# The order of the first loads in a fused linear-attention and gated-FFN kernel: second x tile behind the first key-weight chunk, key products reordered to match

## The chip, the cores and the metric

The kernel runs on one core of a Trainium2 chip, in one launch. The metric is the device time of that launch in microseconds (us). The five engines of a core are named as in the profile: PE (TensorE, with PEld for its weight loads), DVE (VectorE), ACT (ScalarE), POOL (GpSimd) and SP (SyncE, which here only issues transfers). A q after a name (SPq, ACTq, PEq) means that engine's sequencer: instructions that issue a DMA or wait.

## What is computed

Shapes: x is 2048 rows of 640; wqkv is 640 x 1920; wo is 640 x 640; w_gate and w_up are 640 x 1728; w_down is 1728 x 640; all bf16. The part that matters here is the head of the linear-attention block, the projection of keys and queries.

```python
def _A_ref(x, wqkv, wo):                       # 32 heads of 20
    q, k, v = split(x @ wqkv)
    phi = lambda t: where(t > 0, t + 1, exp(t)) + 1e-6
    pq, pk = phi(q), phi(k)
    kv = einsum("bhsd,bhse->bhde", pk, v);  z = einsum("bhsd->bhd", pk)
    o = einsum(pq, kv) / (einsum(pq, z) + 1e-6)
    return o @ wo
def _B_ref(x, w_gate, w_up, w_down):
    return (gelu(x @ w_gate) * (x @ w_up)) @ w_down
g = sigmoid((x * gate_w).sum(-1))
out = g * _A_ref(x, ...) + (1 - g) * _B_ref(x, ...)
```

## The kernel before

The rows of x are cut into 16 tiles of 128 rows, the 640 columns into 5 chunks of 128 (KC = 5). A product of x with a weight needs x transposed (`xT`, one 128 x 128 block per tile and chunk) as the stationary operand and one weight chunk of 128 x 640 as the moving operand. Tiles 2 to 15 of `xT` come by a transposing DMA from SP (`load_xT`, L372). Tiles 0 and 1 are loaded plain (`load_x`, L345) and transposed by PE, so that PE can begin before any transposing DMA has landed.

**Who sets the order.** Each engine runs its own list in the order in which the program text records operations. A small planner, `_Plan`, turns the reads and writes that are declared for each operation into semaphore waits. An engine that waits holds up everything behind it in its list. DMAs are issued from two lists, SP's and ACT's; every load has a semaphore of its own. So the order of lines in the text is the order of the transfers on each queue and the order of the matmuls on PE.

**The loads.** `load_wk(k)` brings key chunk k (160 KB), `load_wq(k)` query chunk k (160 KB), `load_x(i)` x tile i (160 KB). SP issues x tile 0, wk 0, wk 1, wk 3, wq 0, wq 2, wq 4. ACT issues a tiny first DMA (`touch`, L355), x tile 1, then an `Exp` on one column that loads the activation table (L364), then wk 2, wk 4, the gate vector (1.2 KB, into `gw_sb`, which DVE has cleared at L367), wq 1, wq 3. Behind its loads SP issues the transposing loads of tiles 2 to 15; the first of these waits for wk 4 (L378). Then come the large weights of the later stages.

**The start of PE's list** (L502 to L524). `warm(c, n)` runs c matmuls of n columns on constants; they write bank 4 and nothing reads them. `T(i, ks, tb)` transposes chunks `ks` of tile i on PE into a PSUM bank and lets DVE copy them into `xT` (L431, L435). `KM(n, ks)` multiplies chunks `ks` of tile n with the key chunks: one matmul of 512 columns (L451) and one of 128 (L452) for each chunk, a "pair" below. Chunk 0 of a tile has a copy of its own, so that `KM(n, [0])` need not wait for the other four. `gate_col()` (L494) is one small matmul that makes the gate vector a column of `wq`. `QM` (L458) does the same as `KM` for queries of tiles 0 and 1. `phi1` and `phi2` are ACT's exponential and DVE's two steps.

```python
            warm(5, 512)
            warm(1, 128)
            T(0, [0], 7)
            T(0, [1, 2, 3, 4], 6)
            warm(6, 128)
            KM(0, [0])
            T(1, [0], 7)
            T(1, [1, 2, 3, 4], 6)
            warm(3, 128)
            KM(1, [0])
```

After these, chunks 1, 2, 3 alternate between the two tiles, then `gate_col()`, then chunk 4. From there on `KQ(i)` (L529) makes keys and queries of tiles 2 to 15 at once (L536, 15 matmuls per tile), `MM` (L586) the products of keys with x, `G` (L686, L697) the gate and up products of the FFN, and `O_tile` (L852, L861) the output.

Of the kernel before, what the change touches and what calls it, by code (L numbers as in the profile page):

```python
# [161 lines left out]
def bass_gated_mix__linear_attn_block__geglu_ffn__prompt_kernel(  # L162
# [63 lines left out]
    with (  # L226
# [8 lines left out]
        with contextlib.ExitStack() as stack:  # L235
            dma_sems = [stack.enter_context(nc.semaphore("s_in%d" % i)) for i in range(n_dma_in)]

            P = _Plan(["pe", "act", "dve", "pool", "sp"])
# [9 lines left out]
            def new_dma_key():  # L248
                k = "in%d" % dma_next[0]
                dma_next[0] += 1  # L250
                return k

            def v16(o, n):
                return pool[:, o:o + n]
# [45 lines left out]
            gw_sb = v16(O_GW, 128)  # L300
# [36 lines left out]
            r_gw = P.res("gw")  # L337

            def dma_in(dst, src, writes, reads=(), eng="sp"):
                P.op(eng, lambda e, dst=dst, src=src: e.dma_start(dst, src),  # L340
                     reads=reads, writes=writes, dma=new_dma_key())
# [3 lines left out]
            def load_x(i, eng="sp"):  # L345
                dma_in(x_aug[:, i, 0:640], A_x[0, i * 128:(i + 1) * 128, :], [r_xn[i]], eng=eng)

            def load_wk(k, eng="sp"):
                dma_in(wk[:, k, :], A_wqkv[k * 128:(k + 1) * 128, 640:1280], [r_wk[k]], eng=eng)

            def load_wq(k, eng="sp"):
                dma_in(wq[:, k, 0:640], A_wqkv[k * 128:(k + 1) * 128, 0:640], [r_wq[k]], eng=eng)
# [3 lines left out]
                 writes=[P.res("touch")], dma=new_dma_key())  # L356
            load_x(0)
            load_wk(0)
            load_x(1, "act")
            load_wk(1)  # L360
            load_wk(3)

            zero = nc.const_aps.tensor(0.0, (128, 1), F32)
            P.op("act", lambda e: e.activation(eg[:, 0:1], zero, ACT.Exp), writes=[r_eg[0]])  # L364
            load_wk(2, "act")
            load_wk(4, "act")
            P.op("dve", lambda e: e.memset(gw_sb, 0.0), writes=[r_gw])  # L367
            dma_in(gw_sb[0:5, :], gate_w.rearrange("(k p) -> k p", p=128), [r_gw], eng="act")
            for k in range(KC):
                load_wq(k, ("sp", "act")[k % 2])  # L370

            def load_xT(i, after=()):  # L372
                P.op("sp", lambda e: e.dma_start_transpose(xT[:, :, i * 128:(i + 1) * 128],
# [39 lines left out]
            def warm(count, n):  # L413
                def fn(e):
                    last = None
                    for w in range(count):
                        last = e.matmul(ps[:, 4, 0:n], one_l, one_r[:, 0:n], start=True, stop=True)  # L417
                    return last
                P.op("pe", fn, writes=[bank[4]])
# [4 lines left out]
            def slot(n):  # L424
                return SLOTS[n % 4]

            def T(i, ks, tb):
                def fn(e):
                    last = None
                    for n, k in enumerate(ks):  # L430
                        last = e.transpose(psb[:, tb, n * 128:(n + 1) * 128],  # L431
                                           x_aug[:, i, k * 128:(k + 1) * 128], ident)
                    return last
                P.op("pe", fn, reads=[r_xn[i], r_ident], writes=[bank[tb]])
                P.op("dve", lambda e: e.tensor_copy(  # L435
                    xT[:, ks[0]:ks[-1] + 1, i * 128:(i + 1) * 128],
                    psb[:, tb, 0:len(ks) * 128].rearrange("p (k s) -> p k s", k=len(ks))),
                    reads=[bank[tb]], writes=[r_xTa[i] if ks[0] == 0 else r_xT[i]])
# [4 lines left out]
            def KM(n, ks):  # L443
                i = seq[n][1]
                b0, b1 = slot(n)

                def fn(e):
                    last = None
                    for k in ks:
                        lhs = xT[:, k, i * 128:(i + 1) * 128]  # L450
                        e.matmul(ps[:, b0, :], lhs, wk[:, k, 0:512], start=(k == 0), stop=(k == KC - 1))  # L451
                        last = e.matmul(ps[:, b1, 0:128], lhs, wk[:, k, 512:640],  # L452
                                        start=(k == 0), stop=(k == KC - 1))
                    return last
                P.op("pe", fn, reads=[r_xTa[i] if i < NXN and ks == [0] else r_xT[i]] + [r_wk[k] for k in ks],
                     writes=[bank[b0], bank[b1]])
# [37 lines left out]
            def gate_col():  # L494

                P.op("pe", lambda e: e.matmul(ps[:, 7, 0:5], gw_sb, ident[:, 0:5], start=True, stop=True),
                     reads=[r_gw, r_ident], writes=[bank[7]])
                P.op("dve", lambda e: e.tensor_copy(wq[:, :, 640:641], ps[:, 7, 0:5].unsqueeze(2)),
                     reads=[bank[7]], writes=[r_gcol])
# [4 lines left out]
            warm(1, 128)  # L504
            T(0, [0], 7)
            T(0, [1, 2, 3, 4], 6)
            warm(6, 128)
            KM(0, [0])
            T(1, [0], 7)
            T(1, [1, 2, 3, 4], 6)  # L510
            warm(3, 128)
            KM(1, [0])
            for k in (1, 2, 3):
                KM(0, [k])
                KM(1, [k])
            gate_col()
            for k in (4,):
                KM(0, [k])
                KM(1, [k])
            for n in range(4):  # L520
                if n == 2:
                    for k in range(KC):
# [403 lines left out]
```

## Time and profile before

| what | value |
|---|---|
| plain runs, median of 4 | 274.19 us (273.76 to 274.64) |
| profiled execution, its own time | 274.27 us |
| its span, first to last instruction | 273.0 us |
| PE busy | 268.9 us, 98% |
| DVE / ACT / POOL busy | 141.8 / 76.0 / 30.0 us |
| granted TensorE clock, mean | 1.0 |
| first matmul (a constant one) | 0.82 us |
| first transposes of tile 0 / of tile 1 on PE | 3.10 / 4.97 us |
| first key pair, tile 0 / tile 1 | 4.48 / 5.83 us |
| first query matmul / first matmul of `KQ` | 8.48 / 11.20 us |

The issue time of each of the first loads, read from the timeline of its queue, and the time to landing, read from the DMA issues of a window that holds this load alone:

| load | queue, place | issued | to landing |
|---|---|---|---|
| x tile 0 | SP 1 | 0.79 | 2.3 |
| x tile 1 | ACT, behind touch | 1.23 | 3.3 |
| wk 0 | SP 2 | 1.26 | 3.1 |
| wk 1 | SP 3 | 1.71 | 3.7 |
| wk 2 | ACT | 1.78 | 3.8 |
| wk 3 | SP 4 | 2.18 | 3.9 |
| wk 4 | ACT | 2.19 | 4.1 |
| wq 0 | SP 5 | 2.66 | 4.1 |
| gate vector | ACT | 2.69 | not given |
| wq 2 | SP 6 | 3.13 | 4.8 |
| wq 1 | ACT | 3.31 | 4.8 |
| wq 4 | SP 7 | 3.60 | 5.4 |
| wq 3 | ACT | 3.69 | 5.4 |
| xT tile 2 | SP, after wk 4 landed | 6.33 | 3.8 |

How to read it: a load has landed at the sum of the last two columns. A matmul's duration in the profile is longer than the distance to the next one, since matmuls overlap; the pace of PE is read from the distance between starts.

### The profile page before, as it was taken

The numbers are of one execution on the slowest core, as the hardware profiler recorded it, in microseconds if no ns is written. First come the engines' busy times: TensorE is split into PE (matmuls) and PEld (weight loads), VectorE is DVE, ScalarE is ACT, GpSimd is POOL, SyncE is SP. The second block draws the span as 40 slices with busy tenths as digits, with TensorE's granted clock in tenths as the row PEclk, the third lists the DMA queues.
The fourth block names the chain that finished last, engine by engine and source line by source line (L and its number), as shares of the span: only waits on it lengthen the run. The fifth ranks groups of instructions, "written<-read, shape, count | busy, mean of one in ns | idle before, by whom it ended". The sixth has DMA issues, their size and how long they took to land.

```text
span 273.0 us, 3426 instructions
## 1 busy us (share of the span) xinstructions
PE 268.9 (98%) x1343; PEld 129.1 (47%) x1369; DVE 141.8 (52%) x251; ACT 76.0 (28%) x132; POOL 30.0 (11%) x28
## 2 busy tenths in 40 slices
PE   8999999999999999999999999999999999999997
PEld 5555555544445444444444444444444444444444
DVE  2598988998234334999999999634210000000200
ACT  2455554310421453223222223224011121121021
POOL 5000000003240001242332422000000000000000
DMA  7876999500300011522221221263031110110211
GB/s 232 166 107 120 341 402 383 130 3 11 66 19 2 23 50 50 184 43 48 26 48 24 48 43 33 58 206 119 5 77 38 41 38 19 38 41 19 58 58 41
DMA packets 42208, 23.61 MB, mean 86 GB/s; under 512 B 31567, under 2 KB 40783, under 8 KB 42063
## 3 DMA queue, kind: packets, MB, share of 16 engines
q1 hardware_dynamic: 41429, 22.56, 31.2%
q10 hardware_dynamic: 762, 0.82, 0.8%
q8 instruction: 11, 0.18, 0.3%
q14 instruction: 6, 0.05, 0.1%
HBM read 13.83 MB, written 2.63 MB: 60 GB/s over the span
## 4 chain that ended last, share of the span: by engine, by line
PE 96%; DVE 2%; issue 1%; ACT 1%; DVEq 0%; ACTq 0%
PE ps L697 41%; PE ps L861 23%; PE ps L536 12%; PE ps L593 6%; PE ps L840 4%; PE ps L808 2%; PE ps L675 2%; PE ps L596 2%; PE ps L417 1%; PE ps L451 1%; PE ps L821 1%; PE ps L466 1%; DVE pool L490 1%; PE ps L718 1%; DVE pool L555 1%
## 5 line engine op out<-in xcount | busy, mean ns | idle before, releaser
L697 PE MATMUL ps<-pool 128*128 128x512 bf16 x510 | 113.0, 379 | 0.5
L697 PEld LDWEIGHTS ps<-pool 128*128 128x128 bf16 x520 | 50.5, 98 | 60.0
L861 PE MATMUL ps<-pool 128*128 128x512 bf16 (+2 forms) x300 | 62.4, 366 | 0.3
L703 ACT ACTIVATE pool<-ps 128x512 f32<-128x512 f32 x52 | 31.1, 597 | 73.1 <-PE ps L697 73.1
L705 DVE TENSOR_TENSOR pool<-ps,pool 128x512 bf16<-128x512 f32 x52 | 34.7, 689 | 31.7 <-PE ps L697 30.3
L861 PEld LDWEIGHTS ps<-pool 128*128 128x128 bf16 x306 | 29.2, 98 | 33.4 <-issue 0.4
L536 PE MATMUL ps<-pool 128*128 128x512 bf16 (+1 forms) x206 | 37.9, 343 | 0.2
L844 DVE TENSOR_TENSOR pool<-ps,pool 128x512 bf16<-128x512 f32 x4 | 2.8, 692 | 61.5 <-PE ps L840 61.5
L751 POOL TENSOR_TENSOR pool<-pool 128x640 f32<-128x640 bf16 x16 | 22.5, 1408 | 72.8 <-DVE pool L753 65.7
L868 ACT ACTIVATE pool<-ps,pool 128x512 bf16<-128x512 f32 (+1 forms) x16 | 10.9, 681 | 68.6 <-PE ps L861 68.6
L536 PEld LDWEIGHTS ps<-pool 128*128 128x128 bf16 x210 | 20.5, 98 | 17.5
L555 DVE SCALAR_TENSOR_TENSOR pool<-ps,pool 128x128 bf16<-128x128 f32 (+2 forms) x42 | 25.3, 603 | 2.4
L546 ACT ACTIVATE pool<-ps 128x640 bf16<-128x640 f32 x28 | 19.7, 704 | 18.1 <-DVE pool L555 10.6
L593 PE MATMUL ps<-pool 128*128 128x512 bf16 x76 | 19.2, 379 | 0.1
L761 DVE TENSOR_TENSOR pool<-pool 128x640 bf16<-128x640 bf16 x16 | 13.2, 825 | 0.6
L759 DVE TENSOR_SCALAR pool<-pool 128x32 f32<-128x32 f32 x16 | 12.9, 803 | 0.6
L753 DVE TENSOR_REDUCE pool<-pool 128x32 f32<-128x640 f32 x16 | 13.0, 810 | 0.0
L641 DVE TENSOR_TENSOR pool<-pool 128x640 f32<-128x640 f32 x14 | 11.6, 826 | 0.5
L840 PE MATMUL ps<-pool 128*128 128x512 bf16 x51 | 11.5, 379 | 0.1
L643 POOL PARTITION_ALL_REDUCE pool<-pool x1 | 4.0, 3972 | 61.5 <-DVE pool L641 61.5
L593 PEld LDWEIGHTS ps<-pool 128*128 128x128 bf16 x78 | 7.0, 98 | 7.2
L552 DVE TENSOR_SCALAR pool<-pool 128x640 bf16<-128x640 bf16 x28 | 9.1, 326 | 1.8 <-ACT pool L546 0.4
(70 smaller groups left out, 106.8 us busy)
## 6 DMA issues: line engine op xcount, KB each, us to landing
out_dram<-pool SPq DMA_DIRECT2D x19, 128.0 KB, 1.7
pool<-in_B_w_gate_dram SPq DMA_DIRECT2D x1, 2080.0 KB, 14.1
pool<-in_B_w_up_dram SPq DMA_DIRECT2D x1, 2080.0 KB, 18.8
pool<-in_A_x_dram SPq DMA_DIRECT2D x1, 1280.0 KB, 9.5
pool<-in_B_w_down_dram SPq DMA_DIRECT2D x1, 1120.0 KB, 6.7
pool<-omg_row SPq DMA_DIRECT2D x1, 1024.0 KB, 4.9
pool<-in_A_wqkv_dram SPq DMA_DIRECT2D x6, 160.0 KB, 4.0
pool<-in_A_x_dram SPq DMA_DIRECT2D x1, 960.0 KB, 6.6
```

The source lines that it names most:

```text
L536: last = e.matmul(ps[:, b + p, 0:c1 - c0], xT[:, k, i * 128:(i + 1) * 128], wkq[:, k, c0:c1], start=(k == 0), stop=(k == KC - 1))
L546: P.op("act", lambda e: e.activation(e_buf[m], ps_flat[:, o:o + 640], ACT.Exp), reads=banks, writes=[r_e[m]])
L555: P.op("dve", lambda e, c0=c0, c1=c1: e.scalar_tensor_tensor(dst[:, c0:c1], ps_flat[:, o + c0:o + c1], 1.0 + EPS, e_buf[m][:, c0:c1], ALU. ...
L593: last = e.matmul(ps[:, b, :], pk[i][:, c * 128:(c + 1) * 128], x_aug[:, i, 0:512], start=(i == 0), stop=(i == NT - 1))
L697: last = e.matmul(ps[:, b, :], w[:, k, fc * 128:(fc + 1) * 128], xT[:, k, j * 512:(j + 1) * 512], start=(k == 0), stop=(k == KC - 1))
L703: P.op("act", lambda e: e.activation(ge[n], ps[:, gb, :], ACT.Gelu_apprx_tanh), reads=[bank[gb]], writes=[r_ge[n]])
L705: P.op("dve", lambda e: e.tensor_tensor(hT[fc][:, j * 512:(j + 1) * 512], ps[:, ub, :], ge[n], ALU.mult), reads=[bank[ub], r_ge[n]], write ...
L751: P.op("pool", lambda e: e.tensor_tensor(tmp[n], pq[i], z_b, ALU.mult), reads=[r_pq[i], r_zb], writes=[r_tmp[n]])
L753: P.op("dve", lambda e: e.tensor_reduce(den[n], tmp[n].rearrange("p (h d) -> p h d", h=32), AX.X, ALU.add), reads=[r_tmp[n]], writes=[r_de ...
L761: P.op("dve", lambda e: e.tensor_tensor(pq[i].rearrange("p (h d) -> p h d", h=32), pq[i].rearrange("p (h d) -> p h d", h=32), den[n].unsqu ...
L840: last = e.matmul(ps[:, b, :], wd[:, fc, 512:640], hT[fc][:, j * 512:(j + 1) * 512], start=False, stop=(fc == NFC - 2), skip_group_check=True)
L861: last = e.matmul(ps[:, pb, 0:c1 - c0], lhs, rhs, start=False, stop=(q == len(rows) - 1), skip_group_check=True)
```

## The change

The loads change queue and place. SP now issues x tile 0, wk 0, x tile 1, wk 2, wk 4, wq 1, wq 3; ACT issues touch, the gate vector, wk 1, the `Exp`, wk 3, wq 0, wq 2, wq 4. The clearing of `gw_sb` on DVE is written earlier, but was DVE's first instruction already. On PE the six constant matmuls ahead of `KM(0, [0])` become four, two more follow it, the three ahead of `KM(1, [0])` go away, and chunk 1 of tile 0 takes their place; chunk 1 of tile 1 follows chunk 0 of tile 1. The number of pairs is unchanged, the constant matmuls of 128 columns are fewer by three. What the transposing loads wait for (wk 4) is unchanged, though wk 4 is now on SP.

```diff
             load_x(0)
             load_wk(0)
-            load_x(1, "act")
-            load_wk(1)
-            load_wk(3)
+            P.op("dve", lambda e: e.memset(gw_sb, 0.0), writes=[r_gw])
+            dma_in(gw_sb[0:5, :], gate_w.rearrange("(k p) -> k p", p=128), [r_gw], eng="act")
+            load_x(1)
+            load_wk(1, "act")
+            load_wk(2)
 
             zero = nc.const_aps.tensor(0.0, (128, 1), F32)
             P.op("act", lambda e: e.activation(eg[:, 0:1], zero, ACT.Exp), writes=[r_eg[0]])
-            load_wk(2, "act")
-            load_wk(4, "act")
-            P.op("dve", lambda e: e.memset(gw_sb, 0.0), writes=[r_gw])
-            dma_in(gw_sb[0:5, :], gate_w.rearrange("(k p) -> k p", p=128), [r_gw], eng="act")
+            load_wk(3, "act")
+            load_wk(4)
             for k in range(KC):
-                load_wq(k, ("sp", "act")[k % 2])
+                load_wq(k, ("act", "sp")[k % 2])
...
             T(0, [1, 2, 3, 4], 6)
-            warm(6, 128)
+            warm(4, 128)
             KM(0, [0])
+            warm(2, 128)
             T(1, [0], 7)
             T(1, [1, 2, 3, 4], 6)
-            warm(3, 128)
+            KM(0, [1])
             KM(1, [0])
-            for k in (1, 2, 3):
+            KM(1, [1])
+            for k in (2, 3):
                 KM(0, [k])
                 KM(1, [k])
             gate_col()
-            for k in (4,):
-                KM(0, [k])
-                KM(1, [k])
+            KM(0, [4])
+            KM(1, [4])
```

## The prediction

> **What bounds the kernel now.** I read the page's busy shares first, then the table of stretches over the stages, and then the timelines of the first microseconds.
>
> ```profile
> PE 268.9 (98%) x1343; PEld 129.1 (47%) x1369; DVE 141.8 (52%) x251; ACT 76.0 (28%) x132; POOL 30.0 (11%) x28
> ```
>
> ```profile
> 0.00:3.10 3.10, 2.27 (x6) 0.73 (x7) 0.11 (x1) 1.38 (x2) 2.15 (x8) 1.00 0.36 76
> 3.10:4.48 1.38, 1.36 (x13) 1.11 (x12) 0.65 (x2) 0.11 (x1) 1.19 (x3) 1.00 1.01 344
> 4.48:6.19 1.71, 1.71 (x11) 1.22 (x12) 0.65 (x2) 0.00 (x0) 0.22 (x1) 1.00 1.06 377
> 6.19:8.48 2.29, 2.29 (x20) 1.31 (x19) 0.18 (x1) 0.07 (x1) 0.00 (x0) 1.00 1.13 320
> 8.48:11.20 2.72, 2.67 (x21) 1.54 (x21) 1.99 (x4) 1.29 (x3) 0.00 (x0) 1.00 0.81 117
> 11.20:49.28 38.08, 37.87 (x209) 20.66 (x212) 33.50 (x70) 20.98 (x44) 0.00 (x0) 1.00 0.90 265
> ```
>
> The columns are stretch, length, then busy us of PE, PEld, DVE, ACT and POOL, granted clock, DMA share and GB/s. PE is busy in nearly all of each stretch from 3.10 us on, and the chain that ended last is 96% PE. So the end moves with the moment at which PE has done its first products; whatever PE saves in the first 8.5 us is saved at the end, if nothing later waits for something that did not move. Between 3.1 and 8.5 us the DMA share is full as well (344 to 377 GB/s): the loads come as fast as this case shows they can, and an earlier landing of one is a later landing of another.
>
> PE's own first microseconds:
>
> ```profile
> 3.10 0.71 PE L431 MATMUL ps<-pool 128*128 128x128 bf16 x5
> 3.61 0.85 PE L417 MATMUL ps<-const-bfloat16-1.0 128*128 128x128 bf16 x6
> 4.48 0.59 PE L451 MATMUL ps<-pool 128*128 128x512 bf16 x1
> 4.87 0.31 PE L452 MATMUL ps<-pool 128*128 128x128 bf16 x1
> 4.97 0.74 PE L431 MATMUL ps<-pool 128*128 128x128 bf16 x5
> 5.51 0.52 PE L417 MATMUL ps<-const-bfloat16-1.0 128*128 128x128 bf16 x3
> 5.83 0.56 PE L451 MATMUL ps<-pool 128*128 128x512 bf16 x1
> 6.22 0.22 PE L452 MATMUL ps<-pool 128*128 128x128 bf16 x1
> 6.28 0.38 PE L451 MATMUL ps<-pool 128*128 128x512 bf16 x1
> ```
>
> ```profile
> 4.45 0.10 PEld L451 LDWEIGHTS ps<-pool 128*128 128x128 bf16 x1 [0.27 <-DVE pool L435]
> ```
>
> Three things are to be seen. First, PE runs at half pace until about 6.19 us: the first key pair takes 4.97 - 4.48 = 0.49 us, a pair from 6.28 on takes 0.27 (6.28, 6.55, 6.82). The clock column says 1.00 throughout and does not show this; the starts do. Second, constants fill 3.61 to 4.48 and 5.51 to 5.83, work that nobody reads. Third, the weight load at 4.45 is put down to DVE, but DVE's copy of chunk 0 began at 3.43 and took 0.22; what came last was wk 0, landed at 1.26 + 3.1 = 4.4. The six constants at 0.107 each end at 4.25, so PE stood 0.23 us.
>
> **The loads.** From the table of loads, landings come in pairs, one from each queue:
>
> ```profile
> pool<-in_A_x_dram ACTq DMA_DIRECT2D x1, 160.0 KB, 3.3
> pool<-in_A_wqkv_dram SPq DMA_DIRECT2D x1, 160.0 KB, 3.1
> pool<-in_A_wqkv_dram SPq DMA_DIRECT2D x1, 160.0 KB, 3.7
> pool<-in_A_wqkv_dram ACTq DMA_DIRECT2D x1, 160.0 KB, 3.8
> ```
>
> These are x tile 1, wk 0, wk 1, wk 2. In order of landing: x tile 0 at 3.1, wk 0 4.4, x tile 1 4.5, wk 1 5.4, wk 2 5.6, wk 3 6.1, wk 4 6.3, wq 0 6.8. The two queues share one service, so I count tiles. After the change wk 0 has no rival on ACT until wk 1, which ACT issues behind touch (0.78) and the gate vector (1.23 + 0.59), near 1.87. Alone, the second tile lands between 3.1 (one tile) and 4.5 (three tiles): I take 3.8, bounds 3.5 and 4.4. x tile 1, issued third on SP at 1.71, lands between 4.5 (third to land) and 5.4 (third on SP now): I take 4.95. wk 1 is then the fourth, 5.1 to 5.4; wk 2 and wk 3 5.6 to 6.1; wk 4, now fifth on SP, 6.3 to 6.8 (that place lands at 6.8 now).
>
> [...]
>
> **PE, step by step,** on the profiled execution, with a constant or transpose at 0.107, a cold pair at 0.49, a warm one at 0.27 and the step of the clock left at 6.19:
> - T(0) ends at 3.61 as now; four constants end at 4.03; wk 0 (3.8) and the copy (3.65) are there. KM(0, [0]) 4.03 to 4.52, two constants to 4.73.
> - T(1) waits for x tile 1 until 4.95 and runs from 4.97 to 5.51: by this estimate just where it runs now. The 0.45 us won ahead of it are given back to the load.
> - KM(0, [1]) now stands where three constants stood: 5.51 to 6.00 instead of 5.51 to 5.83. wk 1 is there by 5.4. It also covers DVE's copy of tile 1 chunk 0, which now ends at 5.32 + 0.23 = 5.55; without that cover KM(1, [0]) could start no sooner than 5.6.
> - KM(1, [0]): 0.19 us of it cold (0.39 of the pair), the rest 0.61 x 0.27 = 0.17, end 6.36 against 6.28 now.
> - Behind it seven pairs remain, against eight now: -0.27. Sum: +0.08 - 0.27 = -0.19 us.
>
> The bounds of the unknown load: with x tile 1 at 4.5, T(1) starts at 4.73, 0.24 us of cold time earlier, worth half: -0.31. With it at 5.4, T(1) ends at 5.94, KM(0, [1]) at 6.32, KM(1, [0]) at 6.59: +0.31 - 0.27 = +0.04. At 6.1, SP's fourth place now, T(1) ends at 6.41 and the two pairs at 6.95: +0.67 - 0.27 = +0.40. If only wk 0 stays at 4.4, T(1) starts at 5.18: -0.09.
>
> Edits with no price: the gate vector is issued 1.46 us sooner and is used at 7.9. DVE's memset (0.87 to 0.98) is done before ACT reaches the DMA that waits for it (1.23). The table load (1.71, 1.28 us) slips behind two DMA issues, under 1 us, and the first exponential is at 8.41. The query chunks keep their places in each queue within one: wq 1 and wq 3, now sixth and seventh on SP, land near 8.0 and 9.0 by those places and are used near 8.8 and 9.9; wq 0, wq 2 and wq 4 on ACT near 6.8, 8.1 and 9.1, used at 8.3, 9.3 and 10.4.
>
> SP's queue behind wk 4 needs a look: it holds all transposing loads and the large weights. The first transposing load starts at 6.33, when wk 4 is there, and lands 3.8 us later, at 10.1; KQ(2) needs it at 11.20. Shifted by up to 0.5 it lands at 10.6 against a need at 11.0. Later tiles come every 1.3 us, KQ takes 2.7 per tile. No cost, with 0.4 us to spare. The keys' chain on ACT and DVE (first exponential at 8.41) starts with the end of the key pairs and moves with it.
>
> So the profiled execution becomes 274.27 - 0.19 = 274.08; it is 0.08 above the median of the plain runs, so the forecast for the median is 274.0.
>
> **Rivals.** A is the forecast.
>
> B: the order does not do what it says. x tile 1, third in its queue, lands at 5.4 to 6.1, PE waits for it, and the sum is +0.04 to +0.40: 274.2 to 274.6. For it: the third SP load lands at 5.4 now. Against: until 1.87 nothing but small transfers is issued on ACT.
>
> C, slower: SP's wait for wk 4 holds the transposing loads too long. It decides once wk 4 lands later than 7.1. At the seventh SP place now (9.0) the first tile lands at 12.8 and KQ(2) stands 1.8 us: 275.8. Against: wk 4 is issued fifth, and that place is at 6.8.
>
> D, slower: PE's full pace comes later. It came 5.4 us after the first matmul (0.82), with one hole of 0.23 us. If the wait ahead of T(1) (0.22 by my sum, more under B) makes that count begin again at 4.97, the step is at 10.4, and 4.2 us of matmuls run at half pace: +2.1, 276.1. It counts as slower once the step is later than 8.2. Against: PE waited as long at 4.25 and the step still came. [...]
>
> E, faster: with fewer holes and more real work PE's step comes sooner. At 4.48, the first pair, the 1.71 us to 6.19 would be done in half: -0.85, in sum -1.05, 273.1. It counts as faster once the step is before 4.95. For it: the plain runs spread over 0.88 us, which fixed loads do not explain. Against: constants keep PE just as busy now.
>
> **How the numbers follow.** 0.3%, about 0.8 us, is what a measurement of this kernel can tell from no change. A and B, -0.31 to +0.40, lie within it whole: A 0.55, B 0.16, together 0.71. E has 0.13, D 0.12, C 0.04: faster 0.13, slower 0.16. The range runs from E's 273.1 to 274.2 + 0.40 + 0.4 for the scatter of executions (half of 0.88), 275.0; it leaves out C and D. The likeliest case's own range is 273.5 to 274.6.
>
> **What would show it.** Right: KM(0, [0]) near 4.0, T(1) near 5.0 with a short wait for x tile 1, no constants between T(1) and KM(0, [1]), the first query matmul near 8.3 instead of 8.48, KQ(2) with no wait. Wrong: T(1) at 5.4 or later (B), a matmul of KQ waiting for a DMA near 11 us (C), pairs still 0.49 us apart after 7 us (D), or 0.27 us apart before 5 us (E).

## The result: slower by 0.29%

The changed kernel takes 274.52 us (median of 39 runs, 274.17 to 276.95) against 273.96 us (64 runs, 273.48 to 275.78); the ratio is 1.0029, 95% interval 1.002 to 1.0039. Nearly no change was forecast (274.0), with 0.71 on a difference too small to measure.

The times have two parts. 31 of the 39 runs lie between 274.17 and 275.02, median 274.42; eight lie between 276.21 and 276.95. Of the 64 runs of the kernel before none is over 276. The mean of all 39 is 274.87, that of the 31 alone 274.45, that of before 274.06. So of the 0.80 us by which the mean rose about half (0.39 us) lies in the common executions, and the other half (0.41) comes from one execution in five that is 2.0 us longer than the rest.

The profiled execution took 274.20 us, span 272.9. It is no slower than the profiled one of before (274.27), and its trace must be read with that in mind. Three stretches of the changed kernel (stretch, length, busy us of PE, PEld, DVE, ACT, POOL, granted clock, DMA share, GB/s):

```profile
3.10:4.48 1.38, 1.31 (x15) 1.01 (x13) 0.65 (x2) 0.61 (x2) 1.19 (x3) 1.00 0.93 225
4.48:6.19 1.71, 0.79 (x9) 0.51 (x9) 0.52 (x2) 0.00 (x0) 0.22 (x1) 1.00 1.00 346
6.19:8.48 2.29, 2.29 (x18) 1.21 (x17) 0.31 (x2) 0.24 (x1) 0.00 (x0) 1.00 0.93 327
```

PE is busy 0.79 of 1.71 us between 4.48 and 6.19; in the kernel before it was busy all of that time. The DMA rate in the stretch ahead of it is 225 GB/s instead of 344. The timeline of PE, and who ended its waits over the whole span:

```profile
3.08 0.71 PE L431 MATMUL ps<-pool 128*128 128x128 bf16 x5
3.59 0.43 PE L417 MATMUL ps<-const-bfloat16-1.0 128*128 128x128 bf16 x4
3.87 0.38 PE L451 MATMUL ps<-pool 128*128 128x512 bf16 x1
4.08 0.22 PE L452 MATMUL ps<-pool 128*128 128x128 bf16 x1
4.13 0.28 PE L417 MATMUL ps<-const-bfloat16-1.0 128*128 128x128 bf16 x2
5.40 0.45 PE L431 MATMUL ps<-pool 128*128 128x128 bf16 x5 [0.99 <-DMA pool<-in_A_x_dram]
5.69 0.38 PE L451 MATMUL ps<-pool 128*128 128x512 bf16 x1
...
8.31 0.38 PE L466 MATMUL ps<-pool 128*128 128x512 bf16 x1
```

```profile
PE ps L431 <- DMA pool<-in_A_x_dram: 1.0, 1, 1.0
PE ps L417 <- PEq L912: 0.8, 1, 0.8
```

KM(0, [0]) starts at 3.87, ahead of the 4.03 that was expected, and then PE stands for 1.0 us until x tile 1 lands. The issue at 1.71 takes 3.7 us to landing, 5.4:

```profile
pool<-in_A_x_dram SPq DMA_DIRECT2D x1, 160.0 KB, 3.7
```

The pace shows a second thing: the pair at 3.87 takes 0.26 us, so in this execution PE was at full pace before 3.9 us, against 6.19 in the one profiled before. That gain is not the change's: a kernel below ("Filling the hole") has the same loads and the same instructions on PE up to this pair, and there the pair, at 4.01, takes 0.53 us. The gain hides the hole when the two profiles are put side by side. The first query matmul comes at 8.31 against 8.48.

That start time carries everything. Each profiled execution's own time less the start of its first query matmul (L466 here) is 265.79 for before (274.27 - 8.48), 265.89 for the changed kernel, and 265.79 to 265.89 in eleven of the experiments below; the two exceptions are named there. So nothing behind 8.5 us gained or lost.

### The profile page after: what moved, and what is told of

The parts are those of the page before. It is cut to its first block, busy times and chain, and to the rows that moved or that the text cites. A ratio compares the mean times of both kernels' runs of the same rounds, so it can differ in the third digit from the quotient of the medians.

```text
span 272.9 us, 3420 instructions
## 1 busy us (share of the span) xinstructions
PE 267.8 (98%) x1340; PEld 128.0 (47%) x1366; DVE 141.8 (52%) x251; ACT 76.0 (28%) x132; POOL 30.0 (11%) x28
## 4 chain that ended last, share of the span: by engine, by line
PE 97%; DMA 1%; issue 1%; SPq 0%; DVE 0%
PE ps L698 41%; PE ps L862 23%; PE ps L537 14%; PE ps L594 6%; PE ps L841 4%; PE ps L809 2%; PE ps L676 2%; PE ps L597 1%; DMA pool<-in_A_x_dram 1%; PE ps L451 1%; PE ps L822 1%; PE ps L466 1%; PE ps L719 1%; PE ps L737 0%; SPq L340 0%
```

## Experiments

Theory L: x tile 1, third on SP, lands late and PE stands for it. Theory C: in some executions that hole also costs PE a stretch at half pace. Rivals: P, the new order on PE; G, the early gate vector; X, loads that are later in some executions. Ratios are to the kernel before, run beside them.

**The two halves of the change.** The changed kernel with the old loads (first run) and with PE's old order (second run):

```diff
 # first: loads as before, PE's list as changed
+            load_x(1, "act"); load_wk(1); load_wk(3)      # and the rest as before
 # second: loads as changed, PE's list as before
+            warm(6, 128); KM(0, [0]); T(1, ...); warm(3, 128); KM(1, [0]); ...
```

> The changed kernel with the order of loads of before and the new order on PE. Theory L (x tile 1 lands late because it is third on SP's queue; PE stands for it): the loads carry the whole loss, so this one runs like before, 273.8 to 274.1 us, T(1) starts near 5.2, and no execution near 276.5. Theory P (the new order on PE is what costs, with key chunk 1 of tile 0 ahead of tile 1's chunk 0): 274.4 us and again a fifth of the executions near 276.5.

> The changed kernel with the new order of loads and PE's order of before (six and three constant matmuls). Theory L: slower than before by 0.4 to 0.8 us in the mean, since T(1) still waits for x tile 1 until about 5.4 us; KM(0, [0]) ends near 4.5 to 4.8, so the hole ahead of T(1) is 0.5 to 0.9 us. Theory P: like before, 273.9.

Old loads: 274.00 us, ratio 0.9997 (0.9986 to 1.0008), longest 274.93. Old order on PE: 274.53, ratio 1.0018 (1.0004 to 1.0031), one of 12 over 276. The loads carry the loss, P falls. PE with the old loads:

```profile
4.27 0.58 PE L451 MATMUL ps<-pool 128*128 128x512 bf16 x1
4.65 0.30 PE L452 MATMUL ps<-pool 128*128 128x128 bf16 x1
4.75 0.31 PE L417 MATMUL ps<-const-bfloat16-1.0 128*128 128x128 bf16 x2
4.90 0.44 PE L431 MATMUL ps<-pool 128*128 128x128 bf16 x5
5.32 0.39 PE L451 MATMUL ps<-pool 128*128 128x512 bf16 x1
...
7.80 0.38 PE L466 MATMUL ps<-pool 128*128 128x512 bf16 x1
```

No idle time is noted on any of them, T(1) starts at 4.90 instead of 5.40, and the first query matmul comes at 7.80: 0.51 sooner than in the changed kernel, and the execution took 273.68, 0.52 less. Here full pace came only near 4.9 us, later than in the profile of the changed kernel, and it still won.

**One load moved back.** x tile 1 second on ACT, ahead of the gate vector; all else as changed:

```diff
+            load_x(1, "act")
             dma_in(gw_sb[0:5, :], ..., eng="act")
-            load_x(1)
             load_wk(1, "act")
```

> The changed kernel with one load moved: x tile 1 goes from third on SP to second on ACT, as before, ahead of the gate vector; all else is new. Theory L: x tile 1 lands near 4.6 and wk 1 near 5.4, the hole of 1 us ahead of T(1) shrinks to under 0.4, the time is 273.7 to 274.0 and no execution is near 276.5. Theory G (the early gate vector, five short rows, holds up ACT's queue and with it everything): the loss stays, 274.4 or more.

276.60 us, ratio 1.008 (1.0049 to 1.011), where theory L had 273.7 to 274.0. The hole ahead of T(1) is gone (T(1) starts at 5.01), but wk 1, now fourth on ACT and issued at 2.33, takes 5.3 us, and PE stands 2.1 us ahead of KM(0, [1]). This profile shows a fall of the clock behind a hole. Its stretches from 5.37 us, and PE's wait and some starts:

```profile
5.37:8.78 3.41, 1.31 (x12) 0.67 (x11) 0.64 (x2) 0.00 (x0) 0.00 (x0) 1.00 0.87 293
8.78:12.20 3.42, 3.42 (x16) 1.77 (x15) 0.39 (x2) 0.95 (x2) 0.00 (x0) 0.50 0.94 151
12.20:16.00 3.80, 3.80 (x26) 2.00 (x25) 2.63 (x6) 1.78 (x5) 0.00 (x0) 1.00 0.59 119
```

```profile
7.73 0.39 PE L451 MATMUL ps<-pool 128*128 128x512 bf16 x1 [2.10 <-DMA pool<-in_A_wqkv_dram]
...
8.28 0.38 PE L451 MATMUL ps<-pool 128*128 128x512 bf16 x1
8.50 0.22 PE L452 MATMUL ps<-pool 128*128 128x128 bf16 x1
8.55 0.40 PE L451 MATMUL ps<-pool 128*128 128x512 bf16 x1
...
8.85 0.63 PE L451 MATMUL ps<-pool 128*128 128x512 bf16 x1
9.27 0.31 PE L452 MATMUL ps<-pool 128*128 128x128 bf16 x1
9.38 0.63 PE L451 MATMUL ps<-pool 128*128 128x512 bf16 x1
```

PE was busy in 1.31 of 3.41 us; for the next 3.4 us the granted clock (the column behind POOL's) is 0.50, though PE is busy throughout. Its pairs go from 0.27 us to 0.53. Half of 3.4 us is 1.7 us. The expectations below call a stretch of this length a window. A smaller hole need not do this: in the profiled execution of the changed kernel PE reached full pace before 3.9 us; in the 3.42 us from 3.66 on, which hold the hole of 1.0 us, it was busy 2.43, and the clock stayed at 1.00:

```profile
3.66:7.08 3.42, 2.43 (x24) 1.38 (x22) 1.07 (x3) 0.06 (x1) 0.92 (x3) 1.00 0.99 329
```

This run is one exception above (266.19): half pace lasted past the first query matmul, 11.54.

**The gate vector.** Three runs: it alone moved behind wk 3 in the changed kernel; the same in the kernel just shown; and it alone moved up, right behind x tile 1, in the kernel before.

```diff
-            dma_in(gw_sb[0:5, :], ..., eng="act")          # third or second on ACT
             load_wk(3, "act")
+            dma_in(gw_sb[0:5, :], ..., eng="act")          # the third run: the reverse, in the kernel before
```

> The changed kernel with one transfer moved: the gate vector's goes behind wk 3 on ACT, near its old place; x tile 1 stays third on SP, PE's order stays new. Theory L (the third place on SP makes x tile 1 late): it lands at 5.2 to 5.5 again, the hole ahead of T(1) stays near 1 us, 274.4 us in the common executions. Theory G (the early gate vector slows the loads that follow it: behind it single rows of 1280 bytes were seen to take 0.5 to 1.4 us, and the DMA rate in 3.1 to 4.5 us fell from 344 to 225 GB/s): x tile 1 lands by 4.8, the time is 273.6 to 274.0, no execution near 276.5.

> The kernel that ran at 275 to 277.7 us (x tile 1 second on ACT, gate vector third, wk 1 fourth) with the gate vector moved behind wk 3; nothing else. Theory G: 273.7 to 274.0, wk 1 lands by 5.5. Theory L2 (wk 1 behind x tile 1 on ACT is what is late there): 275 or more again, with PE standing ahead of KM(0, [1]).

> The kernel before with one transfer moved: the gate vector's goes from behind wk 4 to right behind x tile 1 on ACT. Everything that PE needs first is issued ahead of it. Theory G: the loads behind it (wk 1 to wk 4) land later and scatter, and the time rises by 0.4 us or more, with some executions over 276. Theory L: 274.0 as before, at most 0.1 more since wk 2 and wk 4 are issued 0.5 us later.

Late in the changed kernel: 275.09, ratio 1.0056 (1.0033 to 1.0079), five of 12 over 276; x tile 1 lands at 1.71 + 3.9 = 5.6. So G does not explain the late tile: wk 1, issued at 1.23, lands ahead of it, at 4.5. Late with x tile 1 on ACT: 274.30, ratio 1.0015 (0.9998 to 1.0033), one of 12 over 276; this lies between what the two theories gave, and in its profile PE still waits 0.3 us for wk 1. Early in the kernel before: 274.41, ratio 1.0019 (1.0007 to 1.0032): wk 2 is issued at 2.40 instead of 1.78, lands at 6.7 instead of 5.6, and PE waits 0.6 us for it:

```profile
6.70 0.39 PE L451 MATMUL ps<-pool 128*128 128x512 bf16 x1 [0.59 <-DMA pool<-in_A_wqkv_dram]
```

An early gate vector does cost, by the 0.6 us that ACT spends on issuing it (1.72 to 2.33) and by what then queues. In the changed kernel it stood ahead of wk 1, not of x tile 1.

**The exchange alone.** The kernel before with x tile 1 and wk 1 exchanged, nothing else:

```diff
-            load_x(1, "act")
-            load_wk(1)
+            load_wk(1, "act")
+            load_x(1)
```

> The kernel before with two loads exchanged and nothing else: x tile 1 third on SP, wk 1 second on ACT. Theory L: x tile 1 lands near 5.4 where wk 1 landed, T(1) starts 0.5 to 0.9 us later behind a hole, and the time is 0.3 to 0.8 us over before, with some executions over 276. Rival (what hurts is the early gate vector or the later wk 4, not the exchange): within 0.1 us of before.

276.21 us, ratio 1.0095 (1.0065 to 1.0126); the six runs go from 274.12 to 278.03, four over 276, and two (277.32, 278.03) have a mean granted clock of 0.994. The exchange alone makes the loss, and a larger one than the whole change makes. In its profiled execution, the quickest, x tile 1 lands at 5.2 and PE waits 0.3 us for it; none of the long ones was profiled.

**No rival on ACT.** All seven first loads on SP in the order of need, ACT's loads held until x tile 1 has landed:

```diff
+            # in short form
+            for load: x 0, wk 0, x 1, wk 1, wk 2, wk 3, wk 4      # all on SP
+            dma_in(gw_sb..., reads=[r_xn[1]], eng="act"); load_wq(0..4, "act")
```

> The changed kernel with all seven first loads on SP in the order of need (x tile 0, wk 0, x tile 1, wk 1, wk 2, wk 3, wk 4); ACT issues its table load, and the gate vector and the query chunks only after x tile 1 has landed. PE's order is the changed one. Theory S (x tile 1, third on SP, is late because wk 1 on ACT takes half of the service while it is under way): without a rival it lands by 4.5 and the hole ahead of T(1) is gone, wk 1 lands near 5.0; 273.6 to 274.2. Theory I (the third place itself, issue and first bytes, is what is slow): it lands at 5.2 or later, 274.4 or more.

x tile 1 lands at 1.71 + 3.1 = 4.8 and T(1) runs from 4.80 with no hole, against 5.4 with wk 1 beside it: sharing costs it 0.6 us. That is the direction of theory S, which had said 4.5. Two third loads on SP agree: 4.7 in the kernel before with the gate vector early, 5.0 with x tile 1 on ACT, where ACT issues its next large load, behind x tile 1, only at 2.40 and 2.33. As a kernel it is worse, 275.52, ratio 1.0055 (1.0031 to 1.0078), three of eight over 276; the query chunks come late and QM waits 1.0 us for them (the second exception above). T(1), and the DMA rate:

```profile
4.80 0.73 PE L431 MATMUL ps<-pool 128*128 128x128 bf16 x5
```

```profile
3.10:4.48 1.38, 1.38 (x12) 1.09 (x11) 0.65 (x2) 0.00 (x0) 1.18 (x3) 1.00 0.91 262
```

With only SP's loads under way the rate between 3.1 and 4.48 us is 262 GB/s. In the three profiles with the changed kernel's loads, where ACT's first large load is issued at 1.84, it is 206 to 240. With that load issued at 1.23 it is 307 to 354 in nine profiles and 257 in a tenth. A high rate does not bring x tile 1 sooner, though: with the exchange it is 333, with the gate vector late 335, and x tile 1 lands at 5.2 and 5.6, since wk 1 lands ahead of it there, at 4.3 and 4.5. The row with the gate vector late:

```profile
3.10:4.48 1.38, 1.20 (x12) 0.91 (x11) 0.65 (x2) 0.11 (x1) 1.19 (x3) 1.00 1.01 335
```

**Filling the hole.** Constants in place of the hole, with the loads untouched: in the changed kernel (eight instead of two), with the gate vector late (twelve instead of two), and in the exchange (twelve instead of none).

```diff
             KM(0, [0])
-            warm(2, 128)
+            warm(8, 128)        # 12 in the second and third
             T(1, [0], 7)
```

> The changed kernel with eight constant matmuls instead of two ahead of T(1); nothing else. x tile 1 lands as late as before. Theory C (the executions near 276.5 are those in which the hole ahead of T(1) keeps PE's clock at half for longer): the common executions stay at 274.3 to 274.5, but the ones near 276.5 become rare or vanish, the mean falls by about 0.4. Theory X (they come from the transposing loads behind wk 4, not from PE's clock): a fifth of the executions stay near 276.5.

> The kernel with the gate vector late (5 of its 12 executions were over 276 us) with twelve constant matmuls instead of two between KM(0, [0]) and T(1). The loads are the same, x tile 1 lands near 5.6 again. Theory C (an execution over 276 is one in which the hole ahead of T(1) lets PE's clock fall or stay at half for a window): the constants keep PE busy through the hole where the pace is half, so none or one of the executions is over 276; the others stay at 274.3 to 275.4. Theory X (those executions have later loads): five of twelve again.

> The kernel before with x tile 1 and wk 1 exchanged (four of its six executions were over 276 us) and twelve constant matmuls between KM(0, [0]) and T(1), where it had none. The loads are those of the exchange, x tile 1 lands at 5.2 to 5.6. Theory C (the long executions come from PE's clock, which falls or stays at half when PE stands in a window): no execution over 276, the median falls from 276.2 to between 274.2 and 274.8, the hole left there costs only itself. Theory X (the long executions are those with later loads): the spread of 274 to 278 stays.

| loads | unfilled, over 276 us | filled, over 276 us | filled, median and ratio |
|---|---|---|---|
| changed kernel | 8 of 39 | 0 of 11 | 274.50, 1.0014 (1.0002 to 1.0026) |
| gate vector late | 5 of 12 | 0 of 12 | 274.67, 1.0026 (1.001 to 1.0042) |
| exchange | 4 of 6 | 1 of 12 | 274.80, 1.0025 (1.0008 to 1.0042) |

Work that nobody reads makes the kernels quicker: of 57 executions 17 were over 276, of 35 only one is (275.91 is the next), and the rest stay about where they were, since x tile 1 is as late as ever (5.8, 5.8 and 5.6 in the profiles). Only PE's constants differ between filled and unfilled, so theory C holds and X falls as the main cause, with two reserves. Filled and unfilled kernels did not run beside each other, and PE's old order on the changed loads, unfilled, had only one of 12 over 276. And loads do vary: wk 2, issued at 2.18 in both, lands at 6.3 in the profile of the changed kernel and at 7.6 in that of the filled one, the longest of its executions, where PE waits for it (last line):

```profile
4.01 0.63 PE L451 MATMUL ps<-pool 128*128 128x512 bf16 x1
4.44 0.26 PE L452 MATMUL ps<-pool 128*128 128x128 bf16 x1
4.54 0.63 PE L417 MATMUL ps<-const-bfloat16-1.0 128*128 128x128 bf16 x8
...
7.64 0.39 PE L451 MATMUL ps<-pool 128*128 128x512 bf16 x1 [0.41 <-DMA pool<-in_A_wqkv_dram]
```

**A hole elsewhere.** The kernel before without its six and three constants:

```diff
-            warm(6, 128)
-            warm(3, 128)
```

> The kernel before without the six and three constant matmuls of 128 columns behind the transposes; loads as before. PE then stands from 3.6 to about 4.4 us and again for 0.3 us ahead of KM(1, [0]), 1.1 us together against 0.23 before; no work that is needed moves. Theory C (holes in the first microseconds keep PE's clock at half for longer in some executions): the common executions stay at 273.6 to 274.6 and some, a tenth or more, are 1.7 to 2.2 us longer. Rival to C (holes cost only themselves): 274.0 with none over 275.5.

Median 273.97, ratio 1.0007 (0.9989 to 1.0025), two of 12 at 275.6 and 275.7, none over 276. In common executions the holes cost nothing, as wk 1 sets the pace there (in the profile PE waits 0.19 us for it, until 5.82); the two longer ones agree with C but are too few to prove it.

**A try for a faster version.** The old loads with the changed order on PE, without ACT's tiny first DMA:

```diff
-            P.op("act", lambda e: e.dma_start(touch[0:16, 0:4], ...))
```

> The kernel with the old loads and the new order on PE (274.0 us, as before), without the tiny first DMA on ACT: x tile 1 is then ACT's first, issued near 0.8 instead of 1.23. A try for a faster version. If loads share one service by count, x tile 1 lands near 3.8 and x tile 0 a little later than 3.1, T(1) starts 0.3 to 0.5 us sooner, wk 1 sets the pace next: 273.6 to 273.9. If ACT's first DMA starts slowly whatever it is, nothing is won: 274.0.

275.06 us, ratio 1.0046 (1.0023 to 1.0069), four of 12 over 276. Both x tiles land close together (0.79 + 2.8 = 3.6 and 0.78 + 3.0 = 3.8), so T(0) starts 0.5 us later, with a hole ahead of it:

```profile
3.63 0.71 PE L429 MATMUL ps<-pool 128*128 128x128 bf16 x5 [0.41 <-DMA pool<-in_A_x_dram]
```

No version tried beats the kernel before.

## Why the prediction failed

The sum gave -0.19 us; the median rose by 0.56. That 274.52 lies in rival B's 274.2 to 274.6 is in part luck: B reaches so far by a landing of up to 6.1, and for the landing seen, 5.4, it has 274.2.

**The term that was mis-sized: x tile 1's landing.** The prediction took 4.95 us, between 4.5 and 5.4; the profile shows 5.4, and the other runs with this place and wk 1 on ACT 5.2 to 5.8. The count of tiles assumed that the service runs at one rate whichever queue feeds it, and the prediction read the loads as coming at full rate from 3.1 to 8.5 us ("344 to 377 GB/s"; its own third row has 320). Between 3.1 and 4.48 us the changed kernel ran at 225 GB/s, not 344: (344 - 225) x 1.38 us = 164 kB, one tile of 160 KB less by that time. Where the rate was high, in the exchange and with the gate vector late, wk 1 came first and x tile 1 was as late. What these runs share is the third place on SP with wk 1 on ACT; why the rate is low when ACT's large load comes later stays open. Rival B named this landing and its row, the third SP load at 5.4, and should have been the forecast.

**The price of that landing was too low as well.** At 5.4 us the sum gave +0.04; the common executions lost 0.46 (274.42 - 273.96). The sum was made on one profiled execution in which PE went to full pace at 6.19, so that a hole ahead of 6 us was charged at half. That moment is not the kernel's: it was before 3.9, near 4.9 and 6.19 in three profiles. The profile of before was one of its slower executions, 274.27 against a lowest of 273.48. Where full pace comes early, half pace hides none of the hole. No profile shows the kernel before with early full pace; if the lowest times are such executions, the price is 274.17 - 273.48 = 0.69. Also, DVE's copy of chunks 1 to 4 of tile 1 was given no price; at full pace it has one:

```profile
5.95 0.10 PEld L451 LDWEIGHTS ps<-pool 128*128 128x128 bf16 x1 [0.16 <-DVE pool L435]
...
6.37 0.10 PEld L451 LDWEIGHTS ps<-pool 128*128 128x128 bf16 x1 [0.31 <-DVE pool L435]
```

These are the weights of tile 1's chunks 0 and 1, each behind DVE's copy. The second wait shows on PE: the pairs of the two chunks start at 5.96 and 6.37, 0.41 us apart instead of 0.27.

**Rival D came near in size, but was wrong in kind.** It gave +2.1 for full pace coming late, as one outcome with 0.12 on it. It is a share of the executions: 8 of 39 are 2.0 us longer than the rest. That moves a mean by 0.41 and the median of all runs by 0.1. The nearness of 2.1 and 2.0 is in part luck: D let a count of 5.4 us begin again at 4.97, which no run shows. No profile of a long execution of the changed kernel itself was taken; the clock of 0.994 in the longest (276.95; 0.6% of 273 is 1.6 us), the 0.50 in the experiment's stretch and the fills are the evidence. The other seven have a mean clock of 1.0, so no fall of the clock is recorded in them. A late first step would not show there, as the clock column reads 1.00 in the half-pace stretches of the profile before; that they had one is likely, not shown.

**What held.** wk 0 without a rival landed at 1.26 + 2.3 = 3.6 (3.8 expected, bounds 3.5 and 4.4). The gain ahead of T(1) was given back to the load, as the sum said, and then more. C did not happen: wk 4 landed at 2.65 + 4.2 = 6.9, the first transposing load started at 6.9, took 3.0 us and KQ(2) waited for nothing. E did not happen as a change; full pace came early in the kernel before too, with only the gate vector moved (its first pair, at 4.31, takes 0.27 us). The tail behind the first query matmul moved by 0.1 us at most.

**The two queues and the clock.** Two equal loads exchanged between the queues cost 0.95% here, and 0.48 us of later issue became 0.7 us of later landing (4.5 to 5.2, one profile each): at the start of this kernel the queue and the place in it matter. One queue alone moved 262 GB/s between 3.10 and 4.48 us where two moved 206 to 354, so these runs do not show that a single queue is the slower way. Full pace came at different times in different executions, also with the same loads and the same instructions ahead (a pair of 0.26 us at 3.87, of 0.53 us at 4.01). What sets that moment, and why the stretch at 0.50 lasted 3.42 us, no run shows.

## What to carry to other kernels

Read a load's landing from its place in its queue beside what the other queue carries; a count of tiles gave 4.95 us here, where 5.4 was measured. At the start of a kernel price a hole on PE twice: once at full pace (here 0.46 us in the common executions), and once as the chance of a longer execution (here 8 of 39, by 2.0 us). One profile shows one moment of full pace (before 3.9, near 4.9 and 6.19 us in three), so compare two profiles by a moment behind the start (here the first query matmul) and look at the spread of the runs before believing a sum made on either.

## What was not expected of the hardware

A stretch in which PE was busy 38% (1.31 of 3.41 us) was followed by 3.4 us at half clock with PE fully busy; a stretch with 71% (2.43 of 3.42) was not. With about 1 us of waiting in the first 6 us one execution in five of the changed kernel (8 of 39) was 2 us longer; with eight constant matmuls in the hole instead of two none of 11 was, and of all 35 filled executions one was over 276 us. With ACT's first large load issued at 1.23 us the DMA rate at 3.1 to 4.48 us was over 300 GB/s in nine of ten profiles; with it issued at 1.84 it was 206 to 240 in three. A tiny DMA ahead of ACT's first large load was worth more than the 0.45 us it takes: without it x tile 0 landed 0.5 us later and the kernel took 0.46% longer.
